# Rounding copies of the experts' weight tiles: from three quarters on GpSimd to all on ScalarE

## The chip, the core and the metric

The kernel runs on one core of a Trainium2 chip. A core has five engines, each with a queue of its own that it works through in order: TensorE (PE in the rows, with PEld for its weight loads), VectorE (DVE), ScalarE (ACT), GpSimd (POOL) and SyncE (SP), which here only issues transfers. They meet through semaphores. On-chip memory is SBUF; matmuls write PSUM. The metric is the device time of one execution in microseconds, as the median of several.

## The reference

Three steps follow each other: an attention with a local window and 32 global tokens, a mixture of eight experts, and a dense layer. Cut to what matters here:

```python
# x: (2304, 512), the attention's output as rows of tokens
logits = x @ w_gate                          # (2304, 8)
order = np.argsort(-logits.flatten())        # greedy: best pairs first
for idx in order:                            # each token one expert,
    tok, e = int(idx) // E, int(idx) % E     # each expert 288 tokens
    if assigned[tok] >= 0 or counts[e] >= cap:
        continue
    assigned[tok] = e
    counts[e] += 1
for e in range(E):                           # E = 8, F = 1024
    mask = assigned == e
    h = np.maximum(x[mask] @ w1[e], 0.0)     # (288, 512) x (512, 1024)
    out[mask] = h @ w2[e]                    # (288, 1024) x (1024, 512)
h = out @ w_in                               # (2304, 512) x (512, 2048)
g = np.maximum(h, 0.0) + np.log1p(np.exp(-np.abs(h)))
return g @ w_out                             # (2304, 2048) x (2048, 512)
```

## The kernel before

After the attention (0 to about 205 us) and a set-up, the kernel goes through the experts in eight **turns**. A turn finds one expert's tokens, gathers them, runs them through that expert and through the dense layer, and scatters the rows to the output. Turns two to six take about 78 us each.

Every matmul is made of three. A 32-bit operand is held as a rounded copy (names that end in h: wh, hh, xh, yh, gh) and the residual that the rounding leaves (wl, hl, xl, yl, gl), and `mm3` (L888 to L890) adds h·h, h·l and l·h in PSUM. So every raw weight tile of an expert passes through `wsplit`: a transfer on SP's queue brings `wr` (128x512, four buffers), a **rounding copy** writes `wh` (four buffers), and a subtract on DVE (L883) writes the residual `wl` (four buffers). A turn has 16 such tiles: for each of eight slices f of the hidden width one tile of the first matrix (`wh1_k_f` in the order's names, k the expert's turn counted from 0) and one of the second (`wh2_k_f`). Which engine makes the rounding copy is read from the string `MC["WH"]`, whose letters are used in rotation: "A" is a copy on ACT (L879), any other letter one on POOL (L81, the helper `pcopy`). In the first expert's turn all copies are ACT's whatever the string says.

A turn has two stages.

- **First stage** (`moe1`, 26 us): for each f the matmuls `h` from x and wh1, wl1, then on ACT hh = relu(h) (L923) and on DVE hl, then two f's later the matmuls `acca` from wh2, wl2 and hh, hl. At its end y (yh by ACT, yl by DVE) is what the expert gives.
- **Second stage** (`moe2`, 52 us): sixteen slices f of the dense layer. The matmuls `h2` (shown as h) take y and `wi`; then a softplus: ACT abs (L987) and exp (L988) write sp_e, POOL makes u = e + 1 (L989, shown as sp_u), DVE two operations on sp_e (L994, L995), ACT the logarithm (L996), POOL the add (L1001), ACT the rounding copy gh (L1002), DVE the residual gl (L1003); three slices later the matmuls `accb` (L1032) take gh, gl and `wo`. At the end `ob` goes out with a scatter.

Two other things run inside a turn for the next expert. The **router** (`route`) works on DVE mostly; near the second stage's middle it makes a one-hot table R (L815, two pieces) and small values V (L826), and TensorE forms the token indices from these with 17 small matmuls (`ix`, L831). Small count matmuls (cn, L696) of the router's searches stand in the first stage. And the first four weight tiles of the next expert (f = 0 and 1) are split in this turn's second stage, since four buffers are free by then; the other twelve are split in that expert's own first stage.

The order of instructions on PE, DVE, ACT and POOL isn't written out by hand. A scheduler lays out each engine's queue when the program is built, from the order of the code, the dependences and its own estimate of times. So a copy that changes its engine can move its neighbours too.

Of the kernel before, what the change touches and what calls it, by code (L numbers as in the profile page):

```python
# [41 lines left out]
EARLYC = 12  # L42
CFG = {"order": "adgcm*wnpvbehuqkDxA", "c": 1, "d": 2, "n": 5, "x": 5, "p": 6, "u": 0, "w": 2, "g": [3, 4, 7], "g7": [0, 1, 3], "b": 4, "ps": [1, 2, 2, 3], "pp": 2, "ph": 2, "nb": 2, "xc": 4, "qs": 1, "cv": 3, "k": 1, "r": 15, "m": 0, "e": 0, "h": 1, "z": 4, "uA": 0, "uD": 0, "gD": 0, "gA": 0, "hA": 1, "hD": 1, "nD": 1, "xA": 0, "pD": 1, "cD": 1, "v": [2, 3, 4, 5, 6, 7], "ve": "DPPPPP", "ue": "ADAaaDA", "he": "A", "ge": "DDA"}
NHOP = 6
MC = {"MT0": [0, 1, 3, 5, 10, 11, 12, 14, 15, 17, 20, 21, 24, 25, 26], "MT1": [1, 2, 3, 4, 5, 7, 12, 13, 14, 15, 16, 17, 18, 20, 23], "GT": [24, 1], "GW": 10, "AH": 1, "XB": 8, "HEAD": 4, "L2": "bkadc", "lag": {"a": 0, "b": 1, "c": 2, "d": 3}, "bufs": {"sp_e": 3, "sp_u": 3, "gh": 3, "gl": 4, "wh": 4, "wl": 4, "wraw": 4}, "HT0": "ABhhh", "HT1": "Ahhh", "WH": "PPPA", "WL": "DDDD", "M1L": 2, "H1": 0, "OB": "ADB", "W0": "PPPPPPPD"}
LEFT = CAP - 2 * P


# [5 lines left out]
class K:  # L54
# [553 lines left out]
    def wtile(self, t):  # L608
        return self.mp.tile([P, 512], F32, tag="wraw", bufs=MC["bufs"]["wraw"], name=f"wr{t}")

# [240 lines left out]
    def gather(self, k):  # L851
# [7 lines left out]
        for j, (o, n) in enumerate(self.GR):  # L859
            xg = mp.tile([P, D], F32, tag="row", bufs=3, name=f"xgt{k}_{j}")  # L860
            self.g_ins = nc.gpsimd.indirect_dma_start(out=xg[:n], out_offset=None, in_=self.xs, in_offset=bass.IndirectOffsetOnAxis(ap=idx[:n, j:j + 1], axis=0))
            rows.append(xg)
        for _ in range(MC["GW"]):
            yield
# [8 lines left out]
    def wsplit(self, raw, t, first=False, odd=False, gate=()):  # L873
        nc, mp = self.nc, self.mp
        h = mp.tile([P, 512], F32R, tag="wh", bufs=MC["bufs"]["wh"], name=f"wh{t}")
        l = mp.tile([P, 512], F32R, tag="wl", bufs=MC["bufs"]["wl"], name=f"wl{t}")
        self.wn = getattr(self, "wn", 0) + 1
        if first or MC["WH"][self.wn % 4] == "A":
            nc.scalar.copy(h, raw)  # L879
        else:  # L880
            self.pcopy(h, raw)
        with self.after(*gate):
            (nc.gpsimd if (odd and MC["W0"][self.wn // 2 % 8] == "P" if first else MC["WL"][self.wn % 4] == "P") else nc.vector).tensor_tensor(l, raw, h.bitcast(F32), ALU.subtract)  # L883
        return h, l
# [266 lines left out]
```

## Time and profile before

| what | value |
|---|---|
| median of three runs | 898.28 us (896.85 to 898.62) |
| the profiled execution | 896.36 us, its span in the profile 894.7 us |
| mean granted TensorE clock | 0.942 of full speed |
| turns one to eight end at about | 330, 406, 485, 564, 642, 720, 798 and 895 us |
| first stage / second stage of the fourth turn | 485 to 511 us / 511 to 564 us |

A row of the timeline gives start, duration, engine, line of the kernel, operation and tiles (out<-in), and in brackets how long the engine had been idle before and what released it. Tile names in the profile are without their numbers, so `wh` there is any of the wh tiles. PEclk is the share of its full clock that TensorE was granted.

### The profile page before, as it was taken

The page shows a single profiled execution, that of the slowest core. Times are in us where ns is not written, and L with a number is a line of the kernel's source. Part 1 is how long each engine was busy: PE and PEld are TensorE (multiplying, and loading weights), DVE is VectorE, ACT ScalarE, POOL GpSimd, SP SyncE. Part 2 cuts the span into 40 slices and gives each one's busy share as a digit, 9 for nine tenths or more (in the row PEclk, how much of TensorE's full clock was granted, in tenths as well). Part 3 has the DMA queues.
Part 4 walks back from the last instruction along what each step waited for, and adds up shares of the span by engine and source line. Part 5 has one row for each costly group of instructions (what it writes and reads, how often), then busy time and mean ns, then how long its engine had stood idle before and what let it go on. Part 6 is the DMA issues. An engine that isn't in the chain of part 4 may idle for free.

```text
span 894.7 us, 21024 instructions
## 1 busy us (share of the span) xinstructions
PE 812.1 (91%) x7608; PEld 714.8 (80%) x7608; DVE 666.0 (74%) x1997; ACT 439.7 (49%) x1083; POOL 428.6 (48%) x592
## 2 busy tenths in 40 slices
PE   5689999784499889999999999999999999999996
PEld 3467676563399779989988988997899899889985
DVE  4876778967998968877895887779588778763632
ACT  3575877866635442552454255244525524442542
POOL 6654587720235542653364355336536533642533
PEclk9887999975599989999999999999999999999999
DMA  6997896759630322303031230303123030312000
GB/s 150 232 257 195 239 251 192 252 194 292 210 95 1 95 70 75 95 27 118 2 118 40 81 95 27 119 1 108 55 78 95 26 118 4 118 61 60 1 0 36
DMA packets 128300, 95.76 MB, mean 107 GB/s; under 512 B 62340, under 2 KB 107396, under 8 KB 128196
## 3 DMA queue, kind: packets, MB, share of 16 engines
q1 hardware_dynamic: 125300, 85.50, 33.7%
q0 software_dynamic: 2896, 8.92, 3.0%
q8 instruction: 60, 0.98, 0.4%
q14 instruction: 44, 0.36, 0.1%
HBM read 77.09 MB, written 17.30 MB: 106 GB/s over the span
## 4 chain that ended last, share of the span: by engine, by line
PE 62%; DVE 24%; DMA 4%; issue 4%; SPq 2%; POOL 2%; ACT 2%; POOLq 0%; DVEq 0%; ACTq 0%
PE accb L1032 12%; PE h L888 9%; PE h L890 8%; PE h L889 8%; PE acca L888 4%; PE acca L889 3%; PE acca L890 3%; PE st L407 3%; DVE sp_e L994 3%; DVE R L815 2%; DVE wl L883 2%; DVE gl L1003 2%; PE av L455 2%; PE pt L437 2%; DVE sp_e L995 1%
## 5 line engine op out<-in xcount | busy, mean ns | idle before, releaser
L1032 PE MATMUL accb<-wo,gh 128*128 128x512 f32 x448 | 133.5, 405 | 1.4 <-ACT gh L1002 1.4
L1001 POOL TENSOR_TENSOR sp_u<-sp_u,sp_e 128x256 f32<-128x256 f32 x112 | 89.8, 806 | 85.1 <-DVE sp_e L995 32.4
L888 PE MATMUL h<-yh,wi 128*128 128x256 f32 x448 | 126.3, 287 | 0.2 <-DVE yl L947 0.2
L889 PE MATMUL h<-yl,wi 128*128 128x256 f32 x448 | 126.4, 284 | 0.0
L890 PE MATMUL h<-yh,wi 128*128 128x256 f32 x448 | 126.4, 284 | 0.0
L883 DVE TENSOR_TENSOR wl<-wr,wh 128x512 fp32r<-128x512 f32 x121 | 94.8, 797 | 13.3 <-POOL wh L81 8.2
L81 POOL TENSOR_SCALAR wh<-wr 128x512 fp32r<-128x512 f32 x84 | 59.6, 714 | 82.6 <-PE h L889 49.2
L1032 PEld LDWEIGHTS accb<-wo,gh 128*128 128x128 f32 x448 | 78.5, 192 | 13.3 <-ACT gh L1002 2.3
L888 PEld LDWEIGHTS h<-yh,wi 128*128 128x128 f32 x448 | 85.6, 193 | 4.1 <-DVE yl L947 0.4
L889 PEld LDWEIGHTS h<-yl,wi 128*128 128x128 f32 x448 | 86.5, 193 | 3.1
L890 PEld LDWEIGHTS h<-yh,wi 128*128 128x128 f32 x448 | 86.3, 193 | 3.3
L989 POOL TENSOR_SCALAR sp_u<-sp_e 128x256 f32<-128x256 f32 x112 | 63.8, 574 | 48.7 <-ACT sp_e L988 31.5
L994 DVE SCALAR_TENSOR_TENSOR sp_e<-sp_u,sp_e 128x256 f32<-128x256 f32 x112 | 55.6, 496 | 40.1 <-POOL sp_u L989 40.1
L1032 PE MATMUL accb<-wo,gl 128*128 128x512 f32 x224 | 80.7, 411 | 4.3 <-DVE gl L1003 4.2
L996 ACT ACTIVATE sp_u<-sp_u 128x256 f32<-128x256 f32 x112 | 46.7, 417 | 68.5 <-DVE sp_e L994 67.7
L888 PE MATMUL h<-xh,wh 128*128 128x272 f32 x256 | 76.3, 298 | 0.8 <-DVE xl L871 0.8
L923 ACT ACTIVATE hh<-h 128x272 fp32r<-128x272 f32 x64 | 25.4, 397 | 102.3 <-PE h L890 93.9
L890 PE MATMUL h<-xh,wl 128*128 128x272 f32 x256 | 75.0, 293 | 0.0
L889 PE MATMUL h<-xl,wh 128*128 128x272 f32 x256 | 74.3, 291 | 0.0
L987 ACT ACTIVATE sp_e<-h 128x256 f32<-128x256 f32 (+1 forms) x128 | 49.0, 386 | 44.8 <-PE h L890 44.8
L889 PE MATMUL acca<-hl,wh 128*128 128x272 f32 x256 | 70.3, 289 | 0.0
L890 PE MATMUL acca<-hh,wl 128*128 128x272 f32 x256 | 70.1, 288 | 0.0
(400 smaller groups left out, 2185.4 us busy)
## 6 DMA issues: line engine op xcount, KB each, us to landing
wr<-in_moe_w_dram SPq DMA_DIRECT2D x128, 256.0 KB, 2.8
wraw<-in_moe_w_out_dram SPq DMA_DIRECT2D x16, 512.0 KB, 5.1
wraw<-in_moe_w_in_dram SPq DMA_DIRECT2D x16, 512.0 KB, 4.2
qn<-in_q_l_dram SPq DMA_DIRECT2D x32, 128.0 KB, 3.3
xs_scratch<-xc SPq DMA_DIRECT2D x32, 128.0 KB, 4.0
wout_scratch<-cvs SPq DMA_DIRECT2D x16, 256.0 KB, 4.6
win_scratch<-cvs SPq DMA_DIRECT2D x16, 256.0 KB, 3.9
wo<-wout_scratch SPq DMA_DIRECT2D x16, 256.0 KB, 5.8
```

The source lines that it names most:

```text
L81: self.nc.gpsimd.tensor_scalar(out, in_, 1.0, 1.0, ALU.mult, ALU.mult)
L407: self.pin(nc.tensor.matmul(o, q[:, pr, i].rearrange("p r q -> p (r q)"), kw, start=True, stop=True))
L883: (nc.gpsimd if (odd and MC["W0"][self.wn // 2 % 8] == "P" if first else MC["WL"][self.wn % 4] == "P") else nc.vector).tensor_tensor(l, ra ...
L888: nc.tensor.matmul(ps, wh, ah, start=start, stop=False)
L889: nc.tensor.matmul(ps, wh, al, start=False, stop=False)
L890: nc.tensor.matmul(ps, wl, ah, start=False, stop=stop)
L987: nc.scalar.activation(e, ps, AF.Abs)
L989: nc.gpsimd.tensor_scalar(u, e, 1.0, 1.0, ALU.add, ALU.mult)
L994: nc.vector.scalar_tensor_tensor(e, u, -1.0, e, ALU.add, ALU.subtract)
L996: nc.scalar.activation(u, u, AF.Ln)
L1001: nc.gpsimd.tensor_tensor(u, u, e, ALU.add)
L1032: pe = self.pin(nc.tensor.matmul(t, g[:, cs], w, start=x == 0 and i == 0, stop=x == 15 and i == 2)) if len(fs) > 1 else nc.tensor.matmul(t ...
```

## The change

One string of the table `MC` is different: `"WH": "PPPA"` becomes `"WH": "AAAA"`. In the turns of experts two to eight, twelve of the sixteen rounding copies were POOL's and four ACT's; now ACT makes all sixteen. That is 84 copies of 128x512. They read and write the same tiles with the same buffers, and the subtracts that follow stay on DVE. The line of the table, with all but the changed entry the same:

```diff
-MC = {"MT0": [0, 1, 3, 5, 10, 11, 12, 14, 15, 17, 20, 21, 24, 25, 26], "MT1": [1, 2, 3, 4, 5, 7, 12, 13, 14, 15, 16, 17, 18, 20, 23], "GT": [24, 1], "GW": 10, "AH": 1, "XB": 8, "HEAD": 4, "L2": "bkadc", "lag": {"a": 0, "b": 1, "c": 2, "d": 3}, "bufs": {"sp_e": 3, "sp_u": 3, "gh": 3, "gl": 4, "wh": 4, "wl": 4, "wraw": 4}, "HT0": "ABhhh", "HT1": "Ahhh", "WH": "PPPA", "WL": "DDDD", "M1L": 2, "H1": 0, "OB": "ADB", "W0": "PPPPPPPD"}
+MC = {"MT0": [0, 1, 3, 5, 10, 11, 12, 14, 15, 17, 20, 21, 24, 25, 26], "MT1": [1, 2, 3, 4, 5, 7, 12, 13, 14, 15, 16, 17, 18, 20, 23], "GT": [24, 1], "GW": 10, "AH": 1, "XB": 8, "HEAD": 4, "L2": "bkadc", "lag": {"a": 0, "b": 1, "c": 2, "d": 3}, "bufs": {"sp_e": 3, "sp_u": 3, "gh": 3, "gl": 4, "wh": 4, "wl": 4, "wraw": 4}, "HT0": "ABhhh", "HT1": "Ahhh", "WH": "AAAA", "WL": "DDDD", "M1L": 2, "H1": 0, "OB": "ADB", "W0": "PPPPPPPD"}
```

It is read here:

```python
        self.wn = getattr(self, "wn", 0) + 1
        if first or MC["WH"][self.wn % 4] == "A":
            nc.scalar.copy(h, raw)
        else:
            self.pcopy(h, raw)
```

The scheduler lays the queues out anew. SP's order, and so that of the transfers which bring the tiles, is the same. Three places follow, all in the fourth turn's second stage; names carry turn (3, counted from 0), slice and a buffer number, so `gh_3_5` is slice 5 of this turn's gh, and `wh1_4_0` is slice 0 of the next expert's first matrix.

On ACT, where the first four tiles of the next expert are split (a piece of the difference, + is after the change):

```order
 L988 ACTIVATE sp_e_3_6_8346<-sp_e_3_6_8346 128x256
+L879 CAST wh1_4_0_8759<-wr1_4_0_8757 128x512
 L1002 CAST gh_3_4_8357<-sp_u_3_4_8234 128x256
+L879 CAST wh2_4_0_8765<-wr2_4_0_8763 128x512
+L1002 CAST gh_3_5_8417<-sp_u_3_5_8292 128x256
 L987 ACTIVATE sp_e_3_7_8406<-h2_3_7_8393 128x256
 L879 CAST wh1_4_1_8810<-wr1_4_1_8808 128x512
-L1002 CAST gh_3_5_8417<-sp_u_3_5_8292 128x256
+L879 CAST wh2_4_1_8816<-wr2_4_1_8814 128x512
 L988 ACTIVATE sp_e_3_7_8406<-sp_e_3_7_8406 128x256
 L996 ACTIVATE sp_u_3_6_8347<-sp_u_3_6_8347 128x256
```

Three copies come in between the softplus operations, the fourth ahead of exp of f=7, and gh of f=5 moves ahead of the third copy.

On DVE the same place, first before the change, from gl of f=4 to the first operation on sp_e of f=7:

```order
L1003 TENSOR_TENSOR gl_3_4_8358<-sp_u_3_4_8234,gh_3_4_8357 128x256
L883 TENSOR_TENSOR wl1_4_0_8760<-wr1_4_0_8757,wh1_4_0_8759 128x512
L994 SCALAR_TENSOR_TENSOR sp_e_3_6_8346<-sp_u_3_6_8347,sp_e_3_6_8346 128x256
L803 TENSOR_TENSOR inc_4_8267<-inc_4_8267,rk4_8310 128x34
L995 SCALAR_TENSOR_TENSOR sp_e_3_6_8346<-h2_3_6_8333,sp_e_3_6_8346 128x256
L883 TENSOR_TENSOR wl2_4_0_8766<-wr2_4_0_8763,wh2_4_0_8765 128x512
L883 TENSOR_TENSOR wl1_4_1_8811<-wr1_4_1_8808,wh1_4_1_8810 128x512
L805 SCALAR_TENSOR_TENSOR pos_4_8314<-inc_4_8267,lf_4_8259 128x17
L819 SCALAR_TENSOR_TENSOR tkm_4_8323<-inc_4_8267,lf_4_8259,ts2_4_8266 128x17
L1003 TENSOR_TENSOR gl_3_5_8418<-sp_u_3_5_8292,gh_3_5_8417 128x256
L883 TENSOR_TENSOR wl2_4_1_8817<-wr2_4_1_8814,wh2_4_1_8816 128x512
L994 SCALAR_TENSOR_TENSOR sp_e_3_7_8406<-sp_u_3_7_8407,sp_e_3_7_8406 128x256
```

And after the change:

```order
L883 TENSOR_TENSOR wl1_4_0_8760<-wr1_4_0_8757,wh1_4_0_8759 128x512
L1003 TENSOR_TENSOR gl_3_4_8358<-sp_u_3_4_8234,gh_3_4_8357 128x256
L994 SCALAR_TENSOR_TENSOR sp_e_3_6_8346<-sp_u_3_6_8347,sp_e_3_6_8346 128x256
L883 TENSOR_TENSOR wl2_4_0_8766<-wr2_4_0_8763,wh2_4_0_8765 128x512
L1003 TENSOR_TENSOR gl_3_5_8418<-sp_u_3_5_8292,gh_3_5_8417 128x256
L803 TENSOR_TENSOR inc_4_8267<-inc_4_8267,rk4_8310 128x34
L995 SCALAR_TENSOR_TENSOR sp_e_3_6_8346<-h2_3_6_8333,sp_e_3_6_8346 128x256
L883 TENSOR_TENSOR wl1_4_1_8811<-wr1_4_1_8808,wh1_4_1_8810 128x512
L883 TENSOR_TENSOR wl2_4_1_8817<-wr2_4_1_8814,wh2_4_1_8816 128x512
L805 SCALAR_TENSOR_TENSOR pos_4_8314<-inc_4_8267,lf_4_8259 128x17
L819 SCALAR_TENSOR_TENSOR tkm_4_8323<-inc_4_8267,lf_4_8259,ts2_4_8266 128x17
L994 SCALAR_TENSOR_TENSOR sp_e_3_7_8406<-sp_u_3_7_8407,sp_e_3_7_8406 128x256
```

The same twelve stand there in another order: the subtracts and the gl's stand earlier, the router's small operations later. A little further on, the first operation on sp_e of f=8 now stands ahead of the one-hot R, where it stood behind the router's last operations.

On PE, at the index matmuls of the next expert (a piece of the difference; behind it the sixteen other ix matmuls follow):

```order
 L889 MATMUL h2_3_10_8489<-yl3_8068,wi10_3601 128x256
 L890 MATMUL h2_3_10_8489<-yh3_8067,wi10_3601 128x256
+L888 MATMUL h2_3_11_8521<-yh3_8067,wi11_3603 128x256
 L1032 MATMUL accb3_0_8085<-wo7_3615,gh_3_7_8481 128x512 x2
-L1032 MATMUL accb3_1_8086<-wo7_3615,gh_3_7_8481 128x512
+L1032 MATMUL accb3_1_8086<-wo7_3615,gh_3_7_8481 128x512 x2
 L831 LDWEIGHTS R_4_8321
 L831 MATMUL ix4_8365<-V_4_8328,R_4_8321 128x6
```

One h matmul of f=11 and one accb matmul that stood behind the index matmuls now stand ahead of them.

In the first stage, ACT's queue takes the copies in between the hh activations: for the fourth turn wh1 of f=2, hh of f=0, wh2 of f=2, hh of f=1, wh1 of f=3, hh of f=2 and so on.

## Rows read from the trace of the kernel before

**Rows 1.** The page, part 1: busy time of each engine over the span.

```profile
PE 812.1 (91%) x7608; PEld 714.8 (80%) x7608; DVE 666.0 (74%) x1997; ACT 439.7 (49%) x1083; POOL 428.6 (48%) x592
```

**Rows 2.** Windows: stretch, length, busy by engine (instructions), PEclk, DMA share, GB/s.

```profile
485.00:511.00 26.00, 26.00 (x259) 25.70 (x258) 20.29 (x56) 5.52 (x14) 8.48 (x12) 1.00 0.34 102
511.00:564.00 53.00, 51.03 (x360) 45.27 (x359) 41.49 (x119) 28.20 (x73) 28.55 (x46) 0.97 0.17 51
590.00:642.00 52.00, 49.92 (x363) 44.32 (x362) 41.87 (x119) 27.85 (x72) 28.83 (x47) 1.00 0.18 52
668.00:720.00 52.00, 50.35 (x354) 44.89 (x352) 40.35 (x118) 27.47 (x71) 28.36 (x45) 0.97 0.18 52
541.00:545.00 4.00, 3.73 (x16) 3.44 (x17) 4.00 (x15) 1.71 (x5) 2.60 (x4) 0.58 0.01 2
```

**Rows 3.** Waits of PE, 354 to 798 us: total us, times, longest us.

```profile
PE ix L831 <- DVE R L815: 4.5, 6, 0.8
PE accb L1032 <- DVE gl L1003: 3.7, 8, 0.5
PE ix L831 <- DVE V L826: 2.2, 6, 0.4
```

**Rows 4.** Timeline of PE: start, us, engine, line, tiles, idle before and releaser.

```profile
539.26 0.38 PE L831 MATMUL ix<-V,R 128*128 128x6 bf16 x9 [0.33 <-DVE V L826]
540.39 0.35 PE L831 MATMUL ix<-V,R 128*128 128x6 bf16 x8 [0.75 <-DVE R L815]
541.27 0.80 PE L1032 MATMUL accb<-wo,gl 128*128 128x512 f32 x1 [0.53 <-DVE gl L1003]
```

**Rows 5.** Groups by line: the two kinds of rounding copies of expert tiles.

```profile
L81 POOL TENSOR_SCALAR wh<-wr 128x512 fp32r<-128x512 f32 x84 | 59.6, 714 | 82.6 <-PE h L889 49.2 <-PE acca L890 13.7 <-DMA wr<-in_moe_w_dram 7.5
...
L879 ACT CAST wh<-wr 128x512 fp32r<-128x512 f32 x44 | 27.2, 621 | 49.1 <-PE acca L889 17.5 <-PE h L889 17.2 <-DMA wr<-in_moe_w_dram 12.3
```

**Rows 6.** Timeline of ACT in the fourth turn's first stage.

```profile
486.66 0.40 ACT L923 ACTIVATE hh<-h 128x272 fp32r<-128x272 f32 x1 [1.64 <-PE h L890]
```

**Rows 7.** Timeline of DVE in the fourth turn's second stage.

```profile
528.40 1.22 DVE L883 TENSOR_TENSOR wl<-wr,wh 128x512 fp32r<-128x512 f32 x1
529.92 0.82 DVE L994 SCALAR_TENSOR_TENSOR sp_e<-sp_u,sp_e 128x256 f32<-128x256 f32 x1 [0.30 <-POOL sp_u L989]
...
533.03 0.79 DVE L819 SCALAR_TENSOR_TENSOR tkm<-inc,lf,ts 128x17 f32<-128x17 f32 x1
...
534.07 0.68 DVE L883 TENSOR_TENSOR wl<-wr,wh 128x512 fp32r<-128x512 f32 x1
534.67 0.41 DVE L994 SCALAR_TENSOR_TENSOR sp_e<-sp_u,sp_e 128x256 f32<-128x256 f32 x1
```

**Rows 8.** Timeline of POOL at the same place.

```profile
527.59 0.62 POOL L81 TENSOR_SCALAR wh<-wr 128x512 fp32r<-128x512 f32 x1 [0.18 <-DMA wr<-in_moe_w_dram]
...
529.85 0.61 POOL L81 TENSOR_SCALAR wh<-wr 128x512 fp32r<-128x512 f32 x1
531.39 0.89 POOL L81 TENSOR_SCALAR wh<-wr 128x512 fp32r<-128x512 f32 x1 [0.93 <-DMA wr<-in_moe_w_dram]
532.24 0.84 POOL L989 TENSOR_SCALAR sp_u<-sp_e 128x256 f32<-128x256 f32 x1
```

**Rows 9.** Timeline of ACT at the same place.

```profile
527.18 0.40 ACT L988 ACTIVATE sp_e<-sp_e 128x256 f32<-128x256 f32 x1
...
530.06 0.62 ACT L879 CAST wh<-wr 128x512 fp32r<-128x512 f32 x1 [1.91 <-DMA wr<-in_moe_w_dram]
...
530.90 0.41 ACT L988 ACTIVATE sp_e<-sp_e 128x256 f32<-128x256 f32 x1
```

**Rows 10.** Chain that ended last: last accb matmuls of turns four to six.

```profile
562.36 1.49 PE accb L1032 x6
...
639.77 1.48 PE accb L1032 x6
...
718.18 1.49 PE accb L1032 x6
```

## The prediction

> **What bounds the kernel now.** I read the page's first line, then stretches by stage, the waits, and single engines' timelines. TensorE is busy for 91% of the span and ACT and POOL for half of it [rows 1], so neither the engine that loses the copies nor the one that takes them is the limit as a whole; the question is which wait ends last in each stage. An expert's turn has two. In its first stage (485 to 511 us in the fourth turn) TensorE is busy for 26.00 of 26.00 us at the full clock, 2.4 GHz. In its second it has gaps and a lower clock in some turns: 51.03 of 53 us at 0.97 and 50.35 of 52 at 0.97, but also 49.92 of 52 at 1.00 [rows 2]. The waits say whose fault the gaps are: from the second turn to the seventh TensorE stood 4.5 + 3.7 + 2.2 us for DVE [rows 3]. They fall in one place. The two groups of index matmuls wait 0.33 and 0.75 us for the one-hot tables, and the accb matmul behind them 0.53 us for a residual gl [rows 4]; DVE, whose rows run on without a gap there, is late. So a turn is TensorE's work plus what DVE is late at that place.
>
> **The copies themselves.** 84 copies leave POOL, 59.6 us at 714 ns. ACT makes its 44 at 621 ns [rows 5]; 84 more are 52 us, on an engine that is idle for 51% of the span. Nothing is added on DVE, TensorE or the DMA queues (SP's order is unchanged). Nine of a turn's twelve fall into the first stage, three into the second stage of the turn before.
>
> **First stage.** Nothing can be gained where TensorE has no gap; the copies can only make one. A copy has to wait for a buffer, that is for the h or acca matmuls that read it last, and behind it on ACT now stand the hh activations that the acca matmuls need. I walked one turn through with these rows: eight f's in 26 us, so 3.25 us of TensorE each [rows 2]; 0.62 us for a copy [rows 5], 0.40 for hh, which in the profile starts when h is done [rows 6], 0.68 for DVE's wl [rows 7]. The first one: h of f=0 is done at 486.6, the copy for f=2 ends at 487.2, hh at 487.5 and wl at 487.9. In the new order TensorE reaches the matmul that needs this wl, after h of f=1 (488.0), fourteen small count matmuls, two of h and four of acca, at about 488.9: a second to spare. The second copy of f=2 needs h of f=1 (488.0), so hh of f=1 behind it is done at 488.9; its matmuls come at 491.5. The tightest later places, the copies for f=4 and f=5, keep half a us or more. I price the stage at 0, with bounds of 0 and one copy's 0.62 us for each of eight f's.
>
> **Second stage.** Here DVE is late, and the copies touch it in two ways. Its rows from 528.40 show wl at 1.22 us and the softplus operation sp_e at 0.82, where the same two at 534.07 and 534.67 take 0.68 and 0.41 [rows 7]. At the long ones POOL is at work, in its adds, its L989 or a copy [rows 8]. And POOL's own queue is longer by the copies: sp_e at 529.92 has waited 0.30 us for POOL's u of f=6 [rows 7], which had a copy ahead of it.
>
> The Trainium skill ("SBUF — State Buffer", Who interferes with whom) says that a DVE operation with two inputs in SBUF and a GpSimd operation that reads SBUF take one port in turn, the later one blocked until the earlier ends, while ACT waits for neither. The rows agree in kind: sp_e's 0.82 us begins beside a copy. By that rule alone the three copies could hold DVE for at most 3 x 0.62 = 1.9 us a turn; the walk below finds less, since POOL's adds, which stay, hold it too.
>
> The walk, fourth turn. Up to 527.6 nothing changes. On ACT exp of f=6 ends at 527.58 [rows 9]; the first raw tile has landed then, since POOL's copy stops waiting for the transfer at 527.59 [rows 8]. So the first copy ends at 528.2, as on POOL. The second tile's landing has no row: it lies between the first (527.59) and the third (530.06, where ACT's copy waits for it); I take 528.9, near the even pace of the landings (the fourth is there at 531.39), and its copy ends at 529.5. DVE: first wl from 528.25, still beside POOL's add, to 529.3; gl of f=4 to 529.7; sp_e of f=6 to 530.1, its u ready since POOL went to it straight from the add; second wl, POOL now idle, to 530.75; gl of f=5 to 531.1, its gh no longer behind ACT's wait for the third tile; the small inc and the second sp_e to 531.5; third wl to 532.1. The fourth copy has to wait for its tile, 531.39, so it ends at 532.0, and this holds exp of f=7 behind it on ACT until then (it began at 530.90). That costs nothing as long as u of f=7 is there when DVE comes to it: POOL did it only from 532.24, and now from about 532.4, for the same 0.84, to 533.25. Fourth wl to 532.75, pos and tkm as before some 1.05 us (tkm alone is 0.79 [rows 7]) to 533.8, and sp_e of f=7 begins at 533.8 in place of 534.67: **0.87 us earlier**. The new order puts one more sp_e (0.34) ahead of the one-hot, so the one-hot R, V and the gl that TensorE waits for come 0.53 us earlier. TensorE also finds one accb matmul and one h matmul more ahead of the index matmuls: 0.25 us (six accb take 1.49 [rows 10]) and half of that for the h, half as wide, so 0.37 us of its work that stood behind the wait. Together **0.90 us** a turn. Bounds: if the second tile lands at 529.85, the latest that the rows allow (POOL's copy began then without a wait), gl of f=5 and all behind it come 0.55 us later, and 0.3 us a turn is left; with no landing in the way at all the three waits, 1.6 us, would go.
>
> The sum: five turns (second to sixth) at 0.90 = 4.5. The seventh, whose index matmuls were already behind that h matmul in the old order, 0.5. The first, whose route runs the same way with wl beside POOL, 0.9 by analogy; I have not walked it. 5.9 in all. The last turn's second stage has no copies.
>
> **The clock.** In four turns, the second, third, fourth and sixth, the second stage's clock reads 0.97, as in the rows of the fourth and sixth; it fell after these waits, to a mean of 0.58 over 541 to 545 us, most of that at the lower level, 1.2 GHz [rows 2]. What it costs is the difference of two turns with the same waits: from the end of the fourth to that of the fifth 639.77 - 562.36 = 77.41 us (clock 1.00 in the second stage), from there to the sixth's 718.18 - 639.77 = 78.41 (0.97) [rows 10]. So 1.0 us each, 4 in all. The waits, 1.6 us a turn, shrink to some 0.7; since the same 1.6 us did and did not bring the fall, I take half of it back, 2 us.
>
> **Sum:** 5.9 + 2 = 7.9 us. The profiled execution took 896.36 us (span 894.7), 1.92 under the median of the three runs, 898.28; the profiled one is the fast end, so I take the sum from the median: **890.4 us**.
>
> **Rivals.**
> *The gain is eaten up* (no change, 898). ACT would be the late one in place of POOL: it now has to wait for each tile's landing in its own order, and exp of f=7, the Ln of f=6 and gh of f=6 stand behind the fourth. For it: that copy already ends 1.1 us after the point at which exp used to begin. Against it: u and gh of f=6 and 7 were held by POOL until 532.24 as well. It decides if landings are half a us later than in the trace, for then DVE waits and 0.3 us a turn, 2 in all, is what is left: 896.3, at the edge of no change.
> *ACT's queue stalls the first stage* (slower). Place: hh or a copy behind a copy that waits for its buffer. For it: twenty-three ACT instructions in 26 us now, 14 [rows 2] and nine, each copy with a TensorE wait of its own, where POOL's copies held nobody; and in the new order h comes before the rest of acca, which asks for wl sooner. Against it: the margins above. It decides once copies and activations come more than half a us later than walked; with three waits of 0.4 us in each of seven turns it costs 8.4 us against 5.9 won and a clock that stays as it is: 901.
> *The clock stays up, and DVE's gain is the larger bound* (884): 1.6 us a turn in seven turns, 11, and with all 4 of the clock 15, of which I would expect nearly all. For it: the fifth and seventh turns show a full clock. Against: sp_e is in the way of the one-hot.
>
> **How the numbers follow.** The walk 0.48, the larger gain 0.14, eaten up 0.20, slower 0.18. The range 884.5 to 899.5 takes in the larger gain and no change, and leaves out the slower case and the far end of the larger one, together under 0.2. The likeliest case's own is 887 to 894.5. About 0.2%, 1.8 us, is what a measurement of this kernel can tell; the walk and the larger gain lie beyond it: faster 0.63, same 0.20, slower 0.17.
>
> **What would show it.** ACT near 490 us busy and POOL near 370. In the fourth turn's second stage the wl subtracts shorter, the one-hot about half a us earlier after exp of f=5, the waits of ix and accb 0.7 us a turn in place of 1.6, and turns of some 77 us. The first stages still without a gap of TensorE, hh waiting for h and not for a copy. I am wrong if TensorE waits for ACT (wh, hh) in the first stage, if DVE has gaps between 528 and 537 us that end with ACT's wh, or if the fourth and sixth turns keep 78.4 us.

## The result and the profile after

The changed kernel took **888.27 us** in the median (885.03 to 891.25, 5 runs), the kernel before 898.42 (896.85 to 899.65, 5 runs): a ratio of **0.988**, 95% interval 0.9853 to 0.9906. The forecast was 890.4, in a range of 884.5 to 899.5. The profiled execution took 885.88 us with a span of 884.2, against 896.36 and 894.7: 10.5 us less in the two profiles.

Part 1 of the page of the kernel after, beside [rows 1]:

```profile
PE 805.6 (91%) x7608; PEld 708.2 (80%) x7608; DVE 650.0 (74%) x1997; ACT 484.1 (55%) x1167; POOL 373.7 (42%) x508
```

84 copies have changed sides: ACT has 44 us more and POOL 55 us less, and DVE has the same 1997 instructions in 16 us less.

Windows of the fourth turn's first stage and of the second stages of turns four, five and six, kernel after (columns as in [rows 2]):

```profile
480.50:506.50 26.00, 26.00 (x267) 25.58 (x266) 18.47 (x51) 10.26 (x22) 2.51 (x2) 1.00 0.35 103
506.50:557.00 50.50, 49.43 (x352) 44.12 (x351) 40.73 (x123) 29.90 (x77) 26.59 (x43) 1.00 0.18 54
583.00:633.30 50.30, 49.23 (x350) 43.86 (x349) 40.82 (x122) 29.58 (x77) 26.72 (x43) 1.00 0.19 54
659.30:709.70 50.40, 49.34 (x351) 43.96 (x350) 40.80 (x122) 29.66 (x77) 26.69 (x43) 1.00 0.18 54
```

The reader is to see two things. TensorE has no gap in the first stage, as before. And PEclk is 1.00 in these second stages, where it was 0.97 in the fourth and the sixth [rows 2]: the lower clock is gone from turns two to seven of this profile. In the first turn it is not: the last 60 us of that turn read 0.94 in the kernel before (first row) and 0.97 in the kernel after.

```profile
271.40:331.40 60.00, 55.07 (x371) 47.39 (x370) 49.57 (x135) 28.16 (x72) 30.42 (x41) 0.94 0.16 49
269.60:329.60 60.00, 54.90 (x373) 46.96 (x373) 49.19 (x141) 29.99 (x77) 29.15 (x42) 0.97 0.15 45
```

The chain that ended last, the last accb row of turns four, five and six, kernel after:

```profile
553.20 1.47 PE accb L1032 x6
...
629.62 1.47 PE accb L1032 x6
...
706.06 1.47 PE accb L1032 x6
```

Turns of 76.42 and 76.44 us, where [rows 10] gave 77.41 (full clock) and 78.41 (lower clock).

TensorE's waits of the kernel after over turns two to seven:

```profile
PE ix L831 <- DVE R L815: 3.5, 6, 0.8
PE accb L1032 <- DVE gl L1003: 2.9, 6, 0.5
PE accb L1032 <- ACT gh L1002: 0.3, 1, 0.3
```

The wait for V (2.2 us in [rows 3]) is gone, that for R went from 4.5 to 3.5 and that for gl from 3.7 to 2.9. They shrank, but two of the three are still there. DVE at the place of [rows 7], fourth turn, kernel after:

```profile
523.84 0.93 DVE L883 TENSOR_TENSOR wl<-wr,wh 128x512 fp32r<-128x512 f32 x1 [0.51 <-ACT wh L879]
...
525.23 0.41 DVE L994 SCALAR_TENSOR_TENSOR sp_e<-sp_u,sp_e 128x256 f32<-128x256 f32 x1
525.56 0.68 DVE L883 TENSOR_TENSOR wl<-wr,wh 128x512 fp32r<-128x512 f32 x1
...
529.11 0.41 DVE L994 SCALAR_TENSOR_TENSOR sp_e<-sp_u,sp_e 128x256 f32<-128x256 f32 x1
```

The first wl takes 0.93 us in place of 1.22, and sp_e of f=6 0.41 in place of 0.82. sp_e of f=7, the last row, begins 48.64 us after the end of the turn before (480.47); before it was 534.67 - 485.11 = 49.56.

### The profile page after: what moved, and what is told of

Its sections match the earlier page's. It is cut to its first block, busy times and chain, and to the rows that moved or that the text cites. A ratio compares the mean times of both kernels' runs of the same rounds, so it can differ in the third digit from the quotient of the medians.

```text
span 884.2 us, 20935 instructions
## 1 busy us (share of the span) xinstructions
PE 805.6 (91%) x7608; PEld 708.2 (80%) x7608; DVE 650.0 (74%) x1997; ACT 484.1 (55%) x1167; POOL 373.7 (42%) x508
## 4 chain that ended last, share of the span: by engine, by line
PE 59%; DVE 23%; DMA 7%; issue 3%; ACT 3%; POOL 2%; SPq 2%; POOLq 0%; DVEq 0%; ACTq 0%
PE accb L1032 12%; PE h L888 8%; PE h L890 8%; PE h L889 7%; PE acca L888 4%; PE acca L889 3%; PE acca L890 3%; DVE sp_e L994 3%; PE st L407 3%; DVE sp_e L995 3%; DMA wraw<-in_moe_w_in_dram 2%; DVE gl L1003 2%; DVE wl L883 2%; PE av L455 2%; PE pt L437 1%
## 5 line engine op out<-in xcount | busy, mean ns | idle before, releaser
L879 ACT CAST wh<-wr 128x512 fp32r<-128x512 f32 x128 | 78.7, 619 | 90.3 <-PE h L889 66.5
L890 PE MATMUL h<-yh,wi 128*128 128x256 f32 x448 | 124.5, 280 | 0.0
L888 PE MATMUL h<-yh,wi 128*128 128x256 f32 x448 | 123.7, 283 | 0.1
L1001 POOL TENSOR_TENSOR sp_u<-sp_u,sp_e 128x256 f32<-128x256 f32 x112 | 95.7, 856 | 59.6 <-DVE sp_e L995 38.4
L883 DVE TENSOR_TENSOR wl<-wr,wh 128x512 fp32r<-128x512 f32 x121 | 87.3, 726 | 33.2 <-ACT wh L879 31.5
L989 POOL TENSOR_SCALAR sp_u<-sp_e 128x256 f32<-128x256 f32 x112 | 60.8, 543 | 80.5 <-ACT sp_e L988 67.3
L889 PEld LDWEIGHTS h<-yl,wi 128*128 128x128 f32 x448 | 84.4, 188 | 3.2
L890 PEld LDWEIGHTS h<-yh,wi 128*128 128x128 f32 x448 | 84.3, 188 | 2.5
L888 PEld LDWEIGHTS h<-yh,wi 128*128 128x128 f32 x448 | 82.9, 188 | 3.6 <-DVE yl L947 0.3
L1032 PE MATMUL accb<-wo,gl 128*128 128x512 f32 x224 | 77.5, 402 | 4.1 <-DVE gl L1003 4.0
L1003 DVE TENSOR_TENSOR gl<-sp_u,gh 128x256 fp32r<-128x256 f32 x112 | 55.2, 493 | 24.3 <-ACT gh L1002 22.9
L1002 ACT CAST gh<-sp_u 128x256 fp32r<-128x256 f32 x112 | 45.1, 402 | 44.3 <-POOL sp_u L1001 44.2
```

What stands on the lines that cost most here:

```text
L888: nc.tensor.matmul(ps, wh, ah, start=start, stop=False)
L889: nc.tensor.matmul(ps, wh, al, start=False, stop=False)
L890: nc.tensor.matmul(ps, wl, ah, start=False, stop=stop)
L989: nc.gpsimd.tensor_scalar(u, e, 1.0, 1.0, ALU.add, ALU.mult)
L1001: nc.gpsimd.tensor_tensor(u, u, e, ALU.add)
L1003: self.h_ins = nc.vector.tensor_tensor(gl, u, gh.bitcast(F32), ALU.subtract)
```

## The experiments

A **turn** below goes from the end of one turn's last accb to the end of the next, on TensorE's timeline of the profiled execution. "Set-up" is where the first index matmuls begin. The runs of the kernel before that stood beside these gave medians of 898.42 (35 runs, 890.27 to 903.5), 898.94 (17) and 899.09 us (18).

| kernel | copies | order | median us (range, runs) | ratio, 95% interval | turns 3, 4, 5, 6 in the profile, us |
|---|---|---|---|---|---|
| before | POOL | old | 898.42 (896.85 to 899.65, 5) | 1 | 78.45, 78.73, 77.41, 78.41 |
| after | ACT | new | 888.27 (885.03 to 891.25, 5) | 0.988 (0.9853 to 0.9906) | 76.43, 76.39, 76.42, 76.43 |
| x_order | POOL | new | 901.14 (897.51 to 910.23, 12) | 1.0051 (1.0017 to 1.0085) | 78.28, 79.46, 78.32, 78.35 |
| x_engine | ACT | old | 893.41 (890.0 to 899.01, 12) | 0.9946 (0.992 to 0.9973) | 76.33, 78.04, 78.04, 78.02 |
| p_second | ACT for f=0, 1 | new | 894.89 (890.43 to 899.09, 12) | 0.9961 (0.9934 to 0.9988) | 77.42, 78.92, 77.23, 77.42 |
| p_first | ACT for f=2 to 7 | new | 899.38 (895.27 to 905.46, 12) | 1.0023 (0.9994 to 1.0052) | 77.27, 78.74, 78.83, 77.65 |
| c_read | ACT, POOL reads | new | 896.65 (893.75 to 903.18, 12) | 0.9983 (0.9955 to 1.0011) | 77.24, 79.15, 78.82, 77.36 |
| c_write | ACT, POOL writes | new | 889.26 (885.53 to 891.71, 6) | 0.9901 (0.9871 to 0.993) | 75.94, 76.44, 76.83, 76.16 |
| f_before | POOL, filled waits | old | 891.59 (887.05 to 893.33, 6) | 0.9921 (0.9891 to 0.995) | 76.84, 77.26, 76.85, 76.89 |
| f_after | ACT, filled waits | new | 887.73 (885.84 to 889.08, 5) | 0.988 (0.9852 to 0.9907) | 76.44, 76.36, 76.44, 76.43 |
| fx_engine | ACT, filled waits | old | 886.02 (884.72 to 891.39, 6) | 0.9853 (0.9824 to 0.9883) | 76.46, 76.47, 76.59, 76.51 |
| fx_order | POOL, filled waits | new | 901.37 (898.48 to 904.55, 12) | 1.0026 (1.0007 to 1.0045) | 78.24, 77.97, 78.25, 78.30 |
| after_again | ACT | new | 889.96 (885.93 to 897.35, 7) | 0.9897 (0.9861 to 0.9933) | 76.46, 76.37, 76.42, 76.44 |
| best1 | ACT, late masking | scheduler's | 889.71 (886.6 to 894.26, 6) | 0.9898 (0.9866 to 0.9929) | 76.51, 76.48, 76.56, 78.06 |

### The engine apart from the order (x_order, x_engine)

The change does two things: it moves 84 copies, and through the scheduler it reorders four queues. Two kernels take these apart. After the whole program is written down, an edge of pure issue order is added between each instruction and the next one on its engine, along the order that the other kernel's build had on TensorE, VectorE and ScalarE; copies that stand on another engine than in that build are left free.

```diff
         k.moe()
+        pin_order(tc, nc, k)
...
+    for seq in json.loads(zlib.decompress(base64.b85decode(ORDER))):
+        seq = [here[n] for n in seq if n in here]
+        seq = [i for i in seq if i.engine == seq[0].engine]
...
+        for a, b in zip(out, out[1:]):
+            tc.add_manual_dep(b, a.name, info, reason="pin")
```

For the order alone:

> The copies stay where they were (twelve of sixteen on GpSimd), and TensorE, VectorE and ScalarE are pinned to the order that their queues have after the change. Theory 1 (the engine pays: VectorE is freed of a GpSimd that reads SBUF beside it and hands u over late): the order by itself brings at most the 0.37 us a turn of TensorE work that stands ahead of the index matmuls, less the 0.34 us of one sp_e more ahead of the one-hot, so nothing: 897 to 900 us. Theory 2 (the order pays): most of the 10 us is here, 888 to 892 us.

It took 901.14 us, 0.5% more than before and a little beyond what theory 1 had. For the engine alone:

> The other half: all copies on ScalarE as after the change, but TensorE, VectorE and ScalarE (its other instructions) pinned to the order of before. Theory 1: VectorE comes 0.5 to 0.9 us a turn earlier to the one-hot, 3 to 5 us over six turns, and the clock gives back 2 or more: 889 to 893 us. Theory 2: 896 to 899 us.

893.41 us, half of the gain and 0.4 us above theory 1's range, and where its clock stayed up, as in the third turn, a turn of 76.33 us, the length that the whole change gives. The engine pays and the order alone costs: theory 1 holds, theory 2 falls. What still parts this kernel from the changed one is seen in its windows, second stages of turns three to five:

```profile
431.60:482.60 51.00, 49.72 (x363) 44.33 (x362) 40.75 (x121) 30.11 (x77) 25.81 (x43) 1.00 0.19 53
507.90:560.60 52.70, 51.26 (x363) 45.71 (x363) 40.72 (x121) 30.52 (x77) 26.57 (x43) 0.97 0.17 52
586.00:638.70 52.70, 51.27 (x363) 45.83 (x362) 40.88 (x121) 30.36 (x77) 26.35 (x43) 0.97 0.18 51
```

The same work, with the same waits of TensorE (1.28 us in each of these turns), takes 1.7 us more with the clock at 0.97 than at 1.00.

### Which copies (p_second, p_first)

```diff
-        if first or MC["WH"][self.wn % 4] == "A":
+        if first or int(t.split("_")[2]) < 2 or MC["WH"][self.wn % 4] == "A":
```

This is p_second; p_first has `> 1` in place of `< 2`. Both have the order of after the change.

> The order of after the change, and only the copies of slices f=0 and 1 (in the second stage of the turn before) on ScalarE; of the other twelve nine stay on GpSimd. Theory 1 (the second stage pays, TensorE has no gap in the first): all of the gain, 886 to 890 us. Rival (a GpSimd freed in the first stage pays as well): nine of the twelve copies are missing, 893 to 897 us.

> The order of after the change, and only the copies of slices f=2 to 7 (in the expert's own first stage) on ScalarE. Theory 1: the same as with all copies at their old engines in this order, 897 to 900 us. Rival (first stage): 889 to 893 us.

p_second missed theory 1: 894.89 us in place of 886 to 890, in the rival's range. Its second stages are those of the changed kernel (50.46 and 50.50 us in turns two and three, as there; the border between the stages is here the start of ACT's first yh), but its first stages take 26.92 us in place of 25.95. TensorE's timeline in the fourth turn's first stage, p_second:

```profile
484.12 0.51 PE L696 MATMUL cn4h<-cmp4h,R 128*128 128x32 bf16 x14
485.23 0.39 PE L888 MATMUL h<-xh,wh 128*128 128x272 f32 x1 [0.60 <-POOL wh L81]
```

And POOL's at the same place:

```profile
482.18 1.05 POOL L1017 DMA_INDIRECT out_dram<-ob,idx  x1 [3.33 <-ACT ob L1015]
483.53 0.98 POOL L1017 DMA_INDIRECT out_dram<-ob,idx  x1 [0.30 <-issue]
484.54 1.21 POOL L81 TENSOR_SCALAR wh<-wr 128x512 fp32r<-128x512 f32 x2
```

In the new order TensorE asks for the tile of f=2 sooner. A copy on POOL stands behind the two scatters of the turn before there and comes 0.60 us late. On ACT it has no scatter ahead. With the old order the first stage takes 25.33 us with either engine (before and x_engine), so the engine matters there only because the new order counts on it. p_first gains nothing (899.38), as theory 1 had it: the gain is made in the second stage.

### Why POOL's copies cost DVE time (c_read, c_write)

Both are the changed kernel with its order pinned, and three instructions more on POOL in each second stage, beside the copies of the three tiles that were POOL's. c_read copies the raw tile to a tile that nobody reads; c_write reads one column of it, so as to stand in the same place, and fills the tile with zeros.

```diff
-        nc, mp = self.nc, self.mp
+        nc, mp = self.nc, self.mp; first or self.dum(raw, t)
...
+        self.extra.append((self.nc.gpsimd.tensor_scalar(d, raw.bitcast(F32), 1.0, 1.0, ALU.mult, ALU.mult).ins, None, "tile"))
```

> The changed kernel with its orders pinned, and three more instructions on GpSimd in each second stage: a copy of the same three raw tiles (128x512) to a tile that nobody reads, so that GpSimd reads SBUF beside VectorE and is busy as before, but nobody waits for the result. If the engines' change pays because VectorE is held while GpSimd reads SBUF, or because u waits behind a copy in GpSimd's queue: a turn of 77.0 to 77.5 us in place of 76.42, 893 to 897 us in all. If it pays because VectorE's subtract no longer waits for a late copy: 76.4 us a turn and 886 to 891 us.

> The same, but the three instructions read one column of the raw tile and then fill the tile with a constant (GpSimd's queue is as busy, and it reads next to nothing). If what counts is VectorE held by GpSimd's reading: a turn of about 76.4 us, 886 to 891 us, and below the run that reads. If what counts is GpSimd's queue: as the run that reads, 77.0 us or more a turn.

896.65 us and 889.26 us: reading gives most of the gain back, 0.8 to 0.9 us in the turns at full clock (77.24 and 77.36) and more where the clock fell (79.15 and 78.82), and writing gives back nothing that can be measured. DVE in c_read, third turn's second stage:

```profile
451.52 0.82 DVE L994 SCALAR_TENSOR_TENSOR sp_e<-sp_u,sp_e 128x256 f32<-128x256 f32 x1 [0.30 <-POOL sp_u L989]
...
452.87 0.83 DVE L1003 TENSOR_TENSOR gl<-sp_u,gh 128x256 fp32r<-128x256 f32 x1
```

POOL in c_read beside them:

```profile
451.45 0.62 POOL L1157 TENSOR_SCALAR dum<-wr 128x512 bf16<-128x512 f32 x1
452.33 1.08 POOL L1157 TENSOR_SCALAR dum<-wr 128x512 bf16<-128x512 f32 x1 [0.27 <-DVE sp_e L994]
```

Two DVE operations of 0.41 us take 0.82 and 0.83, each begun beside a copy that nobody waits for. In c_write, fourth turn, DVE:

```profile
528.68 0.41 DVE L994 SCALAR_TENSOR_TENSOR sp_e<-sp_u,sp_e 128x256 f32<-128x256 f32 x1
529.01 0.68 DVE L883 TENSOR_TENSOR wl<-wr,wh 128x512 fp32r<-128x512 f32 x1
```

And POOL:

```profile
528.86 0.52 POOL L1158 MEMSET dum<- 128x512 bf16 x1
```

The two operations keep their short times beside a fill. So what POOL's copies cost was the reading beside DVE, and not, in a size that shows in the medians, their place in POOL's queue. POOL's queue is no shorter in c_write: a fill took 0.52 us and its one-column read 0.29 in the mean, a copy in c_read 0.74. Turn by turn c_write is not quite the changed kernel: in the second and the fifth turn TensorE waited 0.29 and 0.28 us for a gh, which it did not there, and the second lost its clock (76.35 us against 74.42). Whether that is POOL's queue is open. The Trainium skill ("SBUF — State Buffer", Who interferes with whom) says that an operation of DVE with two inputs in SBUF contends with a GpSimd instruction that reads SBUF and not with one that only writes it; these rows agree.

### What the clock costs (f_before, f_after, fx_engine, fx_order)

24 matmuls of 128x128 on constants are put where TensorE waited, ahead of the index matmuls (4), between their two groups (12) and behind them (8), in turns two to seven. All four have their order pinned.

```diff
+            fill = [nc.tensor.matmul(pi[:, P:2 * P], self.one, self.one, start=j == 0, stop=j == 0).ins for _ in range({0: 4, 9: 12}.get(j, 0) if k > 1 else 0)]
```

> The kernel before with its orders pinned, and in the turns two to seven 24 matmuls of 128x128 on constants beside the index matmuls, 4 and 12 ahead of the two groups and 8 behind, where TensorE waited 0.33, 0.75 and 0.53 us; their result is used by nobody. Theory (the waits bring the lower clock, which costs 1.0 us a turn): PEclk 1.00 in all second stages, turns of 77.4 us in place of 78.4, four of them in the profile: 893 to 896 us, with a smaller spread. Rival (the clock falls for another cause): turns of 78.4 us as before, 898 us or, where the matmuls are in the way, more.

> The same 24 matmuls in the changed kernel. Theory: all runs are as the profiled one of the changed kernel, where no second stage of turns two to seven lost clock: 884 to 887 us with a small spread, against 885 to 891 without them. Rival: 888 us and the spread stays.

f_before took 891.59 us, 7 us less than the kernel before and less than the theory's 893 to 896, by doing more work. Windows of its second stages, turns four to six:

```profile
509.20:561.20 52.00, 51.41 (x388) 45.66 (x387) 41.89 (x121) 28.78 (x74) 28.84 (x46) 1.00 0.18 53
586.50:638.00 51.50, 51.24 (x387) 45.58 (x387) 41.43 (x121) 28.69 (x74) 29.00 (x46) 1.00 0.18 53
663.40:714.90 51.50, 51.23 (x387) 45.53 (x386) 41.37 (x121) 28.75 (x74) 29.13 (x46) 1.00 0.18 53
```

The clock is 1.00 in all of them. The waits themselves were not shortened, only filled: the two groups of index matmuls stand 1.14 us apart, 1.13 before. So the low clock hangs on TensorE standing idle there, and the difference of the two kernels turn by turn is its price: 75.26 - 73.74 = 1.52 us in the second turn, then 1.61, 1.47 and, in the sixth, 1.52, in the four turns that read 0.97 before, 6.1 in all. In the fifth, at 1.00 in both, it is 0.56, so a comparison by fill holds something besides the clock: the fifth turn's second wait for gl is gone in f_before. Two turns of one kernel say the same without a fill: in p_second the third took 77.42 us at 1.00 and the fourth 78.92 at 0.97, with the same waits of TensorE (1.68 and 1.67 us), 1.50 apart.

f_after has hardly such a gain (887.73 against 888.27), as its rival had it: the profiled changed kernel had no low clock left where the fill stands. But its spread is 885.84 to 889.08, that of the changed kernel without the fill 885.03 to 891.25 and 885.93 to 897.35. In some of the latter's executions the clock still falls: the mean granted clock of the whole execution is 0.951 to 0.953 in all five of f_after, and in after_again 0.953 in the one of 885.93 us, 0.941 and 0.940 in those of 894.62 and 897.35.

With the clock kept, the other two:

> All copies on ScalarE, the order of before, and the 24 matmuls beside the index matmuls, so that the clock stays. With them the old engines and order took 891.6 us, the new ones 887.7. If the engines alone bring the 3.9 us between: 887 to 889 us, turns of 76.4 us. If the order has a share: 889 to 891 us.

> The copies where they were before, the order of after the change, and the 24 matmuls. If the order by itself gives nothing or costs what its first stage loses with copies on GpSimd (26.9 us in place of 25.9): 892 to 898 us, turns of 77.0 to 78.3 us. If the order pays: 888 to 890 us.

fx_engine took 886.02 us with turns of 76.46 to 76.59, fx_order 901.37, 3 us above its range, with turns of 77.97 to 78.30 and a last turn of 93.42 us where f_before has 91.93. So with the clock out of the way in turns two to seven the engine brings the whole gain, and the new order without it costs more than it gives. That the new order is worth something with the copies on ACT can't be seen in the medians (887.73 against 886.02).

### A try for more (after_again, best1)

> The changed kernel once more, as the base for the other three on the same chip: 885 to 891 us, turns three to six at 76.4 us where the clock stays.

> The changed kernel with the router's operations that the next turn needs (the masking of the logits, 1.2 us of VectorE ahead of the one-hot) queued behind the one-hot, the scheduler free otherwise. If TensorE's last waits of a turn (0.55 us for R, 0.52 us for gl) stand in VectorE's queue: both shrink or go, 0.5 to 1.0 us in each of six turns, 882 to 885 us. If something else holds the turn then (POOL's u, the scheduler's new order): 886 to 889 us.

```diff
-        onehot(slice(9, NCH))
+        o2 = onehot(slice(9, NCH))
...
         if k < E - 1:
+          with self.after(o2):
```

889.71 us against 889.96: nothing gained. The one-hot begins earlier, 50.93 us after the end of the turn before in place of 51.63 (third turn). But its first piece then meets POOL. DVE in best1, third turn:

```profile
454.89 1.78 DVE L815 TENSOR_TENSOR R<-pos,iota 128x1152 bf16<-128x1152 f32 x1
456.59 0.80 DVE L826 SCALAR_TENSOR_TENSOR V<-g,ts 128x34 bf16<-128x34 f32 x3
```

And POOL's:

```profile
454.71 0.75 POOL L1002 TENSOR_TENSOR sp_u<-sp_u,sp_e 128x256 f32<-128x256 f32 x1 [1.49 <-DVE g L809]
455.42 1.92 POOL L990 TENSOR_SCALAR sp_u<-sp_e 128x256 f32<-128x256 f32 x2
```

The piece takes 1.78 us in place of 1.35, and the three V 0.80 in place of 0.39, while POOL works without a break at L1002 and L990 (the add and u). TensorE's wait for R is 0.75 us, longer than the 0.54 of the changed kernel, that for gl 0.47 in place of 0.52. The scheduler was free here and moved other instructions too, so that POOL alone ate up the gain is read from these rows and not shown.

## Why the prediction was right, step by step

The time lay 2.1 us below the forecast, and the mechanism was the one forecast: DVE was late at the index matmuls, held by POOL's reading, and the copies on ACT free it. But the two terms of the sum were off in opposite ways: of the 10.5 us between the two profiles DVE's part is about 4, not 5.9, and the clock's about 6.5, not 2. That the time came so near the forecast is in part luck.

**The walk of the fourth turn held for DVE, and only in sum for TensorE.** sp_e of f=7 was to come 0.87 us earlier and came 0.92 earlier. The turn was to lose 0.90 us: with the clock kept on both sides it went from 77.26 to 76.36, 0.90. But the three waits of [rows 4] were to go from 1.6 us to 0.7 and went from 1.61 to 1.07 (kernels before and after, without a fill). The rest is a fourth wait, earlier in the same turn, that the walk did not have and that is gone after the change. TensorE in the kernel before:

```profile
534.21 0.73 PE L1032 MATMUL accb<-wo,gl 128*128 128x512 f32 x2 [0.36 <-DVE gl L1003]
```

[rows 3] counts eight waits for gl in six turns, so two such waits were there to be seen. That the two errors cancel in this turn is luck.

**"Five turns at 0.90" failed.** The fourth turn is not like the others. In f_before it is the only one of turns three to six with a wait for an earlier gl (0.32 us), and the third, fifth and sixth gain 0.40, 0.41 and 0.46. The seventh gained 0.41 (0.5 predicted). The second seems to lose 0.66 with the new order (73.74 to 74.40; in fx_engine, with the old order, it kept 73.39), and the first, from set-up to its end, to gain 2.1 (101.96 to 99.87 us), where an analogy had put 0.9. But the second turn holds eight h matmuls more in the new order (0.13 us each): 18 of its own, not 24, stand ahead of the first turn's end, and two of the third's ahead of its own. Work has moved from the first turn to the second, and the two are to be read together: 1.4 us. Part of these may be the clock, since the fill does not stand in the first turn, whose last 60 us read 0.94 in f_before and 0.97 in f_after. In all 4.0 us in place of 5.9, which is also the difference of the medians of f_before and f_after (3.9). TensorE's waits for DVE agree: 10.4 us in [rows 3] and 6.4 after the change (3.5 + 2.9), 4.0 less in turns two to seven.

**"1.0 us each" for the clock, and half of it back, failed on the other side.** The base for the 1.0 was the fifth turn at full clock, 77.41 us, taken to have the waits of the sixth. But it had a second wait for gl, 0.44 us, as the waits of the kernel before between 563.8 and 641.3 us show:

```profile
PE accb L1032 <- DVE gl L1003: 1.0, 2, 0.5
PE ix L831 <- DVE R L815: 0.8, 1, 0.8
PE ix L831 <- DVE V L826: 0.4, 1, 0.4
```

So the price is about 1.5 us a turn (1.4 by these two turns, 1.50 in p_second, 1.7 in x_engine) and 6.1 in four turns, and in the profile all of it came back, not half; the first turn, whose lower clock the prediction left out, got some back too (0.94 to 0.97). By subtraction, 10.5 less 4.0, about 6.5 us are the clock's. That all of it came back was not to be read from the trace of before; the prediction chose a half between two ends. It is also in part the luck of that execution: p_second's fourth turn has the same two waits at the index matmuls as the changed kernel, 0.55 and 0.52 us, and lost the clock.

**The first stage at nothing** was right for the time that TensorE stood: 26.00 of 26.00 us busy. (To the end of its last acca matmul the stage takes 26.66 us in place of 26.44, with eleven more of the small count matmuls in it: work moved there from the second stage.) But the reason was incomplete. ACT's hh doesn't always wait for h now; in the fourth turn one stands behind a copy:

```profile
481.76 0.62 ACT L879 CAST wh<-wr 128x512 fp32r<-128x512 f32 x1 [0.90 <-PE h L889]
482.29 0.39 ACT L923 ACTIVATE hh<-h 128x272 fp32r<-128x272 f32 x1
```

No wait of TensorE followed. And the new order has made the stage depend on the engine, by 0.97 us a turn (p_second).

**The rivals.** ACT as the late one in the second stage: DVE does wait 0.51 us for ACT's first copy (the row at 523.84 above), where before the change its first wl began without a gap. The prediction had named such a gap as a sign of being wrong; it was not one, since sp_e of f=7 came 0.92 us earlier all the same. ACT's queue stalling the first stage: no such wait in turns three to six. The larger bound, all waits gone: 884 was not reached; two waits stayed.

## What to carry to other kernels

A copy on GpSimd is not free because GpSimd is idle half the time: look whether VectorE, beside it, reads two tiles from SBUF at a place where TensorE waits for it, and put the copy on ScalarE if that has room. A wait of about a microsecond on TensorE may cost more in clock than in itself, so price the clock by filling the wait with matmuls, or by two turns of one kernel whose waits have been added up and are equal, not by turns that may differ in another wait. And when a scheduler lays out the queues, run the new engine with the old order and the old engine with the new one before naming a cause.

## What was not expected of the hardware

Useless matmuls made the kernel before 7 us faster (891.59 against 898.94 us), mostly because TensorE's granted clock stayed at 1.00 in the second stages of turns two to seven. And the place where the first index matmuls begin, before any of the moved copies, varied from 224.3 us (x_order) to 233.8 (after_again) between profiled executions, so single runs of one kernel differ by several us; the lengths of turns three to six in the profile at an equal clock agreed within 0.1 us (after, after_again and f_after).
